# Sparse attention with an ELU layer: score blocks in pairs, fills placed in the order, the last tile in three pieces, and zero matmuls during batch 0

## The chip, the cores and the metric

One core of a Trainium2 chip runs the whole program. The metric is the device time of one execution in microseconds, the median of several runs. Engines are named as in the profile: PE (TensorE, its weight loads PEld), DVE (VectorE), ACT (ScalarE), POOL (GpSimd), SP (SyncE).

## What is computed

```python
def attn(q, k, v):                      # (8, 8, 576, 64): batch, heads, tokens, head size
    scores = np.matmul(q, k.transpose(0, 1, 3, 2)) / np.sqrt(64)
    rel = pos[:, None] - pos[None, :]
    local   = (rel >= 0) & (rel < 32)                      # heads 0 to 3
    strided = (rel >= 0) & (pos[None, :] % 32 == pos[:, None] % 32)   # heads 4 to 7
    return softmax(where(mask, scores, -1e9)) @ v
x = attn(q, k, v).transpose(0, 2, 1, 3).reshape(4608, 512)
h = x @ w_in                            # (4608, 2048)
out = where(h > 0, h, exp(min(h, 0)) - 1) @ w_out          # (4608, 512)
```

## The kernel before

**Work.** For each batch, four local and four strided heads are handled as four pairs of heads, called by batch, kind and pair: 0s1 is batch 0, strided, pair 1. Each pair has two score blocks, u = 0 and 1. A block's path: scores (S, PE, line 427, 8 matmuls of 72 columns for strided, 6 of 96 for local), exp (e, ACT, line 434), mask (m, DVE, 441 or 447), values and sums (O, PE, 454 to 499), log of the sums and exp of minus it as reciprocal (n and r, ACT, 525 and 530), and the product into xT (x, DVE, 555), which holds x transposed in four parts of 128 features: parts 2 and 3 come from strided heads, 0 and 1 from local ones.

Batches 0 and 1 get q and k transposed on PE (T, lines 388 and 391, 8 or 16 matmuls) and copied out of PSUM by DVE (c) or ACT (C); later ones by a DMA transpose (X). Two heads of q and of k of batch 0 come as f32 through SP into a stage and are cast (K, line 375: q on DVE, k on ACT).

The layers run in nine chunks of 512 tokens. First layer: 16 blocks of 128 features, each four matmuls of 512 columns (L, line 582), in chunk 0 split in a (parts 2 and 3, strided) and b (parts 0 and 1, local). ELU: exp (h, ACT, 590), clamp (i on DVE, 599, or j on ACT, 597), maximum into g (g, DVE, 608 or 610). Second layer: four tiles of 128 tokens for each chunk, 16 matmuls each, issued in four parts of four (Z, line 616), copied out (o on ACT, q on DVE, 622) and stored (t, SP, 634, one DMA for each run of tokens). One tile, 7.3, is done in two halves of 256 columns at the end (Y and y, lines 638 to 660).

**Order.** ORDER (lines 35 to 143) is a text of tokens; the loop at its end runs one token after the other, and so fixes each engine's instruction order. Semaphores make an instruction wait for its data, and everything behind it on its engine waits too. T.0s0.q.7 is the transposes of q for pair 0s0 into PSUM bank 7; S.0s0.1.01 the scores of block 1 into banks 0 and 1; Z.7.3.1.6 is chunk 7, tile 3, part 1, bank 6. D tokens are loads on POOL's queue (D.wi1.0: the second quarter of w_in, features 512 to 1023; D.wo0: the first quarter of w_out), F tokens fills: F.ms and F.ml build masks on DVE, F.mk on POOL.

Before the order, the program loads the stage, preloads ACT's table, loads the other two strided heads of q and k, and sets constants on DVE: among them ones into both local value buffers vl (lines 308 to 310) and into the strided one vsp (311). The order begins with w.7.42: 42 matmuls of 128 x 128 x 128 on zeros (line 369), into columns that nothing reads.

In batch 0 PE's order is w, T.0s0.q, T.0s0.k, T.0l0.k, T.0s1.k, S.0s0.1, T.0l1.q, S.0s0.0, T.0l1.k, O.0s0.1, T.0l0.q, O.0s0.0, T.0s1.q, six score blocks, six O, T.1s1.q, T.1s0.q, and then six a and the first b, b.0.4. The end is Z.8.3.3, Y.7.3.0, y.7.3.0, Y.7.3.1, y.7.3.1, o.8.3, t.8.3.

Of the kernel before, what the change touches and what calls it, by code (L numbers as in the profile page):

```python
# [15 lines left out]
S = 576  # L16
D = 64
HG = 4
NS = 8
RS = S // NS  # L20
# [4 lines left out]
PRE = STRIDE  # L25
CHUNK = 512
W = S // 2
# [8 lines left out]
w.7.42 D.kl.0 D.ql.0 D.vs.0 K.q.1 D.vl.0 K.q.0 T.0s0.q.7 D.wi2.0 K.k.0 D.qs.1 K.k.1 D.wi1.0 T.0s0.k.6  # L36
c.0s0.k c.0s0.q D.wi3.0 T.0l0.k.5 F.ms T.0s1.k.7 S.0s0.1.01 D.wi0.0 C.0s1.k T.0l1.q.6 e.0s0.1 F.mk
S.0s0.0.23 C.0l1.q m.0s0.1 T.0l1.k.7 D.kl.1 e.0s0.0 O.0s0.1.41 C.0l1.k m.0s0.0 D.ks.1 T.0l0.q.6 c.0l0.k
O.0s0.0.70 C.0l0.q F.ml T.0s1.q.3 n.0s0.0 n.0s0.1 S.0l1.1.56 c.0s1.q r.0s0.1 D.vl.1 e.0l1.1 S.0s1.1.01
V.0 S.0s1.0.23 r.0s0.0 m.0l1.1 S.0l0.1.56 e.0s1.1 e.0l0.1 m.0s1.1 S.0l1.0.01 e.0s1.0 m.0l0.1 S.0l0.0.56  # L40
x.0s0.1 D.ql.1 e.0l1.0 m.0s1.0 O.0l1.1.32 x.0s0.0 e.0l0.0 O.0s1.0.41 n.0l1.1 O.0l0.1.70 m.0l0.0 D.wo0.0
r.0l1.1 m.0l1.0 O.0s1.1.26 n.0s1.0 x.0l1.1 r.0s1.0 O.0l1.0.51 n.0s1.1 x.0s1.0 r.0s1.1 O.0l0.0.63 n.0l0.1
x.0s1.1 n.0l1.0 T.1s1.q.4 D.vs.1 T.1s0.q.0 r.0l1.0 c.1s1.q a.0.7.2 n.0l0.0 a.0.11.1 r.0l0.1 a.0.4.4
C.1s0.q x.0l0.1 a.0.8.3 x.0l1.0 r.0l0.0 a.0.10.7 x.0l0.0 D.wo1.0 a.0.12.5 b.0.4 b.0.8 h.0.4 b.0.10 h.0.8
b.0.11 j.0.4 b.0.7 i.0.8 D.wo2.0 h.0.10 a.0.0.6 g.0.8 a.0.1.0 h.0.7 g.0.4 b.0.1 h.0.11 i.0.10 a.0.6.3
D.wo3.0 h.0.1 i.0.7 b.0.0 j.0.11 g.0.7 b.0.6 h.0.0 b.0.12 g.0.10 j.0.1 a.0.15.4 D.qs.2 g.0.11 a.0.9.7
h.0.12 g.0.1 b.0.9 h.0.6 T.1s0.k.2 i.0.12 h.0.9 b.0.15 c.1s0.k a.0.3.1 i.0.6 j.0.9 b.0.3 D.ks.2 g.0.12
h.0.15 T.1l0.k.2 i.0.0 h.0.3 a.0.2.5 g.0.9 C.1l0.k b.0.2 D.vs.2 g.0.6 a.0.5.0 j.0.3 a.0.13.7 g.0.0 h.0.2
b.0.5 j.0.15 g.0.3 b.0.13 j.0.2 g.0.15 S.1s0.1.23 T.1l0.q.6 e.1s0.1 g.0.2 T.1l1.k.1 D.kl.2 T.1l1.q.4
C.1l0.q c.1l1.k S.1s0.0.23 a.0.14.5 h.0.5 m.1s0.1 Z.0.3.0.6 e.1s0.0 c.1l1.q V.1 h.0.13 T.1s1.k.4 i.0.5  # L50
S.1l0.0.12 c.1s1.k b.0.14 e.1l0.0 m.1s0.0 S.1s1.1.34 m.1l0.0 Z.0.0.0.2 e.1s1.1 g.0.5 h.0.14 S.1s1.0.34
j.0.13 O.1l0.0.10 Z.0.3.1.6 e.1s1.0 g.0.13 m.1s1.1 S.1l1.0.34 i.0.14 Z.0.0.1.2 e.1l1.0 m.1s1.0 n.1l0.0
g.0.14 O.1s1.1.74 r.1l0.0 O.1s0.0.30 m.1l1.0 n.1s1.1 Z.0.3.2.6 x.1l0.0 n.1s0.0 r.1s0.0 r.1s1.1
S.1l1.1.01 x.1s0.0 S.1l0.1.45 e.1l1.1 Z.0.0.2.2 x.1s1.1 e.1l0.1 m.1l1.1 O.1l1.0.73 m.1l0.1 O.1l1.1.54
n.1l1.0 O.1s0.1.10 X.qs.2 n.1l1.1 Z.0.3.3.6 r.1l1.0 r.1l1.1 x.1l1.0 O.1s1.0.43 x.1l1.1 X.ks.2 Z.0.0.3.2
n.1s1.0 n.1s0.1 r.1s0.1 O.1l0.1.75 r.1s1.0 x.1s0.1 Z.0.1.0.3 n.1l0.1 x.1s1.0 r.1l0.1 Z.0.1.1.3 x.1l0.1
W.2 L.1.7.7 D.vs.3 L.1.1.5 X.kl.2 h.1.7 D.ql.2 o.0.3 L.1.0.4 t.0.3 L.1.2.6 h.1.0 j.1.7 i.1.0 L.1.4.1
h.1.1 g.1.0 L.1.6.0 D.qs.3 g.1.7 i.1.1 D.ks.3 L.1.8.4 h.1.6 g.1.1 D.vl.2 h.1.2 L.1.14.7 h.1.4 i.1.2
i.1.6 o.0.0 Z.0.1.2.3 i.1.4 h.1.8 g.1.4 Z.0.1.3.3 h.1.14 g.1.2 D.ql.3 S.2s0.0.12 L.1.10.5 e.2s0.0 j.1.14
m.2s0.0 L.1.5.6 g.1.6 h.1.10 O.2s0.0.12 g.1.14 L.1.3.0 n.2s0.0 i.1.8 g.1.8 Z.0.2.0.7 h.1.5 r.2s0.0  # L60
i.1.10 X.ql.2 Z.0.2.1.7 j.1.5 x.2s0.0 h.1.3 L.1.9.4 o.0.1 i.1.3 g.1.10 S.2s0.1.12 t.0.1 L.1.13.3 e.2s0.1
h.1.9 m.2s0.1 Z.0.2.2.7 t.0.0 h.1.13 g.1.5 O.2s0.1.12 i.1.13 L.1.11.6 X.ks.3 i.1.9 n.2s0.1 g.1.13
Z.0.2.3.7 h.1.11 X.qs.3 r.2s0.1 i.1.11 L.1.12.5 g.1.3 o.0.2 L.1.15.3 g.1.11 h.1.12 x.2s0.1 Z.1.0.0.0
h.1.15 g.1.9 D.ql.4 j.1.12 Z.1.0.1.0 g.1.12 S.2s1.1.12 i.1.15 S.2l0.1.67 S.2s1.0.45 e.2s1.1 Z.1.0.2.0
g.1.15 e.2l0.1 m.2s1.1 S.2l0.0.12 m.2l0.1 S.2l1.0.67 e.2l0.0 Z.1.0.3.0 e.2l1.0 m.2l0.0 O.2l0.1.12 q.1.0
Z.1.2.0.3 e.2s1.0 n.2l0.1 t.1.0 m.2s1.0 Z.1.2.1.3 m.2l1.0 r.2l0.1 O.2l1.0.45 t.0.2 O.2s1.0.67 x.2l0.1
n.2l1.0 Z.1.1.0.0 n.2s1.0 X.ql.3 O.2l0.0.12 Z.1.1.1.0 r.2l1.0 r.2s1.0 x.2l1.0 Z.1.2.2.3 n.2l0.0 D.ks.4
x.2s1.0 S.2l1.1.45 r.2l0.0 D.kl.3 Z.1.1.2.0 e.2l1.1 O.2s1.1.67 Z.1.2.3.3 m.2l1.1 n.2s1.1 x.2l0.0
Z.1.1.3.0 r.2s1.1 O.2l1.1.12 D.qs.4 q.1.1 Z.1.3.0.5 n.2l1.1 D.kl.4 x.2s1.1 Z.1.3.1.5 r.2l1.1 o.1.2
x.2l1.1 S.3s1.0.67 e.3s1.0 S.3s0.1.34 S.3s1.1.01 L.2.2.2 m.3s1.0 W.3 L.2.4.7 h.2.2 e.3s0.1 i.2.2 L.2.9.6  # L70
e.3s1.1 g.2.2 O.3s1.0.34 h.2.4 L.2.0.1 h.2.9 i.2.4 D.vs.4 L.2.11.2 i.2.9 h.2.0 g.2.4 D.vl.3 n.3s1.0
L.2.10.0 m.3s1.1 g.2.9 X.kl.3 r.3s1.0 L.2.3.7 h.2.10 x.3s1.0 L.2.6.6 j.2.0 X.ks.4 i.2.10 h.2.3 g.2.10
O.3s1.1.34 h.2.11 Z.1.3.2.5 g.2.0 h.2.6 L.2.12.0 i.2.11 g.2.11 Z.1.3.3.5 h.2.12 i.2.6 i.2.3 n.3s1.1
L.2.7.2 g.2.3 j.2.12 g.2.6 L.2.1.1 o.1.3 m.3s0.1 L.2.5.7 g.2.12 r.3s1.1 t.1.3 h.2.1 x.3s1.1 S.3s0.0.56
X.qs.4 L.2.8.0 e.3s0.0 i.2.1 h.2.7 m.3s0.0 L.2.13.6 h.2.8 g.2.1 t.1.1 h.2.5 L.2.14.5 i.2.7 h.2.13 g.2.7
X.kl.4 L.2.15.1 j.2.5 i.2.13 i.2.8 h.2.14 O.3s0.0.23 g.2.5 Z.2.1.0.4 n.3s0.0 t.1.2 i.2.14 g.2.8
Z.2.1.1.4 r.3s0.0 X.ql.4 h.2.15 x.3s0.0 Z.2.3.0.7 j.2.15 g.2.13 O.3s0.1.23 g.2.14 Z.2.1.2.4 n.3s0.1
g.2.15 r.3s0.1 S.3l0.0.56 D.qs.5 W.4 Z.2.3.1.7 e.3l0.0 D.vs.5 m.3l0.0 S.3l0.1.01 S.3l1.1.56 e.3l0.1
x.3s0.1 Z.2.3.2.7 D.vl.4 e.3l1.1 m.3l0.1 O.3l0.0.01 Z.2.1.3.4 m.3l1.1 n.3l0.0 O.3l0.1.23 r.3l0.0 D.ks.5
q.2.1 Z.2.0.0.6 D.kl.5 n.3l0.1 x.3l0.0 Z.2.0.1.6 r.3l0.1 O.3l1.1.01 x.3l0.1 Z.2.0.2.6 n.3l1.1 r.3l1.1  # L80
S.4s0.0.23 Z.2.3.3.7 e.4s0.0 x.3l1.1 S.3l1.0.45 S.4s0.1.23 m.4s0.0 S.4s1.1.01 e.4s0.1 Z.2.0.3.6 e.3l1.0
m.4s0.1 Z.2.2.0.3 o.2.3 m.3l1.0 e.4s1.1 q.2.0 O.3l1.0.45 Z.2.2.1.3 n.3l1.0 m.4s1.1 D.ql.5 O.4s1.1.67
r.3l1.0 Z.2.2.2.3 n.4s1.1 x.3l1.0 O.4s0.0.01 Z.2.2.3.3 r.4s1.1 n.4s0.0 x.4s1.1 O.4s0.1.45 L.3.11.2
n.4s0.1 L.3.4.7 r.4s0.0 r.4s0.1 x.4s0.0 L.3.1.6 h.3.11 x.4s0.1 X.ks.5 h.3.4 L.3.2.1 i.3.4 L.3.9.0 g.3.4
h.3.2 t.2.1 j.3.11 i.3.2 S.4s1.0.45 L.3.8.7 h.3.9 g.3.2 X.kl.5 e.4s1.0 g.3.11 L.3.3.1 j.3.9 q.2.2 h.3.1
L.3.13.2 m.4s1.0 t.2.2 h.3.8 i.3.1 O.4s1.0.34 h.3.3 g.3.1 L.3.5.5 t.2.3 n.4s1.0 g.3.9 L.3.0.6 h.3.13
i.3.8 t.2.0 g.3.8 j.3.3 L.3.7.0 h.3.0 i.3.13 X.qs.5 h.3.5 g.3.13 L.3.6.7 j.3.0 g.3.3 L.3.12.2 j.3.5
g.3.0 X.ql.5 r.4s1.0 L.3.10.1 g.3.5 h.3.7 x.4s1.0 Z.3.2.0.6 h.3.6 i.3.7 h.3.12 S.4l0.1.34 g.3.7
Z.3.0.0.5 j.3.6 j.3.12 g.3.6 L.3.14.0 e.4l0.1 h.3.10 Z.3.0.1.5 m.4l0.1 h.3.14 i.3.10 O.4l0.1.34 g.3.12
L.3.15.7 n.4l0.1 i.3.14 g.3.10 Z.3.2.1.6 r.4l0.1 W.5 h.3.15 S.4l1.1.12 x.4l0.1 Z.3.0.2.5 D.vs.6 e.4l1.1  # L90
D.kl.7 j.3.15 m.4l1.1 S.4l1.0.12 S.4l0.0.34 g.3.14 Z.3.2.2.6 e.4l0.0 e.4l1.0 O.4l1.1.34 Z.3.1.0.0
n.4l1.1 m.4l1.0 g.3.15 O.4l1.0.12 r.4l1.1 Z.3.1.1.0 D.ql.6 n.4l1.0 x.4l1.1 Z.3.1.2.0 r.4l1.0 m.4l0.0
Z.3.2.3.6 x.4l1.0 O.4l0.0.34 Z.3.0.3.5 n.4l0.0 D.vl.5 r.4l0.0 S.5s0.0.12 Z.3.1.3.0 e.5s0.0 x.4l0.0
Z.3.3.0.7 m.5s0.0 o.3.1 D.qs.6 o.3.0 O.5s0.0.01 D.ks.6 L.4.7.4 n.5s0.0 D.kl.6 L.4.2.5 o.3.2 r.5s0.0
L.4.3.6 h.4.2 x.5s0.0 L.4.5.3 h.4.3 j.4.2 i.4.3 S.5l1.0.01 L.4.8.2 h.4.5 g.4.3 h.4.7 g.4.2 L.4.1.6 h.4.8
# [51 lines left out]
def kernel(  # L147
# [9 lines left out]
    nc = tc.nc  # L157
# [550 lines left out]
```

## Time and profile before

| | |
|---|---|
| Median of 3 runs | 315.01 us (314.72 to 315.85) |
| Profiled execution | 312.68 us, of it span 310.7 us, mean granted clock 0.974 |
| PE, DVE, ACT, POOL busy | 96%, 71%, 75%, 26% of the span |
| L616 and L582, second and first layer | 135.6 and 132.0 us of PE |
| First L1 matmul, last PE instruction's end | 22.26 us, 305.06 us |
| DMA | 37.59 MB, mean 121 GB/s |

The page cuts the span into 40 slices and gives each engine's busy share in tenths, and the clock that PE was granted. The windows view gives the same for chosen stretches, in us, with the number of instructions in brackets. The timeline has one row for instructions of one kind in a row: start, length, engine, line, operation, how many, and in square brackets the idle time of the engine ahead of them with what ended it. Instructions overlap in a pipeline, so a cost is read from start to start.

### The profile page before, as it was taken

The numbers are of one execution on the slowest core, as the hardware profiler recorded it, in microseconds if no ns is written. First come the engines' busy times: TensorE is split into PE (matmuls) and PEld (weight loads), VectorE is DVE, ScalarE is ACT, GpSimd is POOL, SyncE is SP. The second block draws the span as 40 slices with busy tenths as digits, with TensorE's granted clock in tenths as the row PEclk, the third lists the DMA queues.
The fourth block names the chain that finished last, engine by engine and source line by source line (L and its number), as shares of the span: only waits on it lengthen the run. The fifth ranks groups of instructions, "written<-read, shape, count | busy, mean of one in ns | idle before, by whom it ended". The sixth has DMA issues, their size and how long they took to land.

```text
span 310.7 us, 6213 instructions
## 1 busy us (share of the span) xinstructions
PE 299.0 (96%) x2330; PEld 150.4 (48%) x2330; DVE 219.1 (71%) x422; ACT 234.5 (75%) x421; POOL 79.8 (26%) x107
## 2 busy tenths in 40 slices
PE   6789999999999999999999999999999999999992
PEld 5664544444544445444444454445445544444452
DVE  5467985788579976898398886966797739885200
ACT  3698976687978989998798999987778667843021
POOL 8843320934830065006901640000000000000000
PEclk9569999999999999999999999999999999999998
DMA  8999999999999899666998999603102030100152
GB/s 164 188 206 194 207 207 193 165 165 194 165 167 135 129 209 147 133 163 67 126 174 185 122 87 151 169 14 95 36 1 70 0 101 0 37 0 0 40 165 68
DMA packets 106717, 37.59 MB, mean 121 GB/s; under 512 B 88992, under 2 KB 101888, under 8 KB 106688
## 3 DMA queue, kind: packets, MB, share of 16 engines
q0 software_dynamic: 69600, 19.43, 60.3%
q1 hardware_dynamic: 37008, 17.70, 27.7%
q8 instruction: 18, 0.29, 0.4%
q14 instruction: 11, 0.09, 0.1%
q10 hardware_dynamic: 80, 0.07, 0.1%
HBM read 39.47 MB, written 9.44 MB: 157 GB/s over the span
## 4 chain that ended last, share of the span: by engine, by line
PE 87%; DVE 4%; ACT 3%; DMA 2%; issue 1%; POOL 1%; ACTq 0%; POOLq 0%
PE ps L616 38%; PE ps L582 38%; PE ps L427 4%; DMA ql<-in_q_dram 2%; PE ps L490 2%; PE ps L497 2%; DVE g L608 1%; PE ps L642 1%; ACT e L434 1%; DVE he L599 1%; DVE g L610 1%; PE ps L391 1%; PE ps L470 1%; ACT ln L525 0%; ACT osb L622 0%
## 5 line engine op out<-in xcount | busy, mean ns | idle before, releaser
L616 PE MATMUL ps<-w_out_sb,g 128*128 128x512 bf16 x560 | 135.6, 380 | 0.0
L582 PE MATMUL ps<-xT,w_in_sb 128*128 128x512 bf16 x576 | 132.0, 379 | 0.0
L590 ACT ACTIVATE he<-ps 128x512 f32<-128x512 f32 x144 | 80.4, 596 | 24.7 <-PE ps L582 24.1
L582 PEld LDWEIGHTS <-w_in_sb 128*128 128x128 bf16 x576 | 54.5, 98 | 63.1 <-issue 0.6
L616 PEld LDWEIGHTS <-g 128*128 128x128 bf16 x560 | 50.4, 98 | 53.8 <-DVE g L610 0.4
L610 DVE TENSOR_TENSOR g<-he,ps 128x512 bf16<-128x512 bf16 x89 | 59.5, 683 | 1.3
L555 DVE TENSOR_TENSOR xT<-ps,ln 64x576 bf16<-64x576 f32 (+1 forms) x64 | 42.9, 678 | 23.9 <-ACT ln L530 22.0
L599 DVE TENSOR_SCALAR he<-he 128x512 bf16<-128x512 f32 x89 | 38.3, 439 | 14.6 <-ACT he L590 13.8
L434 ACT ACTIVATE e<-ps 72x576 bf16<-72x576 f32 (+1 forms) x64 | 39.8, 646 | 7.8 <-PE ps L427 6.8
L525 ACT ACTIVATE ln<-ps 64x576 f32<-64x576 f32 (+1 forms) x64 | 36.7, 582 | 8.3 <-PE ps L497 3.8
L608 DVE SCALAR_TENSOR_TENSOR g<-he,ps 128x512 bf16<-128x512 bf16 x55 | 36.9, 682 | 8.4 <-ACT he L597 8.0
L530 ACT ACTIVATE ln<-ln 64x576 f32<-64x576 f32 (+1 forms) x64 | 39.2, 620 | 1.6
L597 ACT ACTIVATE he<-he 128x512 bf16<-128x512 f32 x55 | 33.8, 628 | 2.7 <-DVE g L610 1.2
L236 POOL DMA_DIRECT2D ql<-in_q_dram x24 | 20.0, 840 | 11.6 <-DMA qTl<-ql 9.6
L441 DVE TENSOR_TENSOR pm<-e,mask_s 72x576 bf16<-72x576 bf16 x32 | 14.4, 449 | 9.6 <-ACT e L434 9.4
L622 ACT COPY osb<-ps 128x512 f32<-128x512 f32 x18 | 10.3, 583 | 13.4 <-PE ps L616 10.4
L243 POOL DMA_DIRECT2D kl<-in_k_dram x24 | 17.6, 759 | 7.4 <-DMA w_out_sb<-in_moe_w_out_dram 4.6
L447 DVE TENSOR_TENSOR pm<-e,mask_l 128x576 bf16<-128x576 bf16 x32 | 14.4, 454 | 6.0 <-ACT e L434 5.6
L622 DVE COPY osb<-ps 128x512 f32<-128x512 f32 x17 | 11.6, 688 | 7.1 <-PE ps L616 6.5
L230 POOL DMA_DIRECT2D vs<-in_v_dram x7 | 4.7, 671 | 39.8 <-DVE vsp L562 38.9
L253 POOL DMA_DIRECT2D vl<-in_v_dram x8 | 10.1, 1259 | 8.0 <-PE ps L497 6.6
L490 PEld LDWEIGHTS <-vsp 72*128 72x128 bf16 x192 | 9.2, 98 | 5.1 <-DVE pm L441 0.2
(85 smaller groups left out, 161.4 us busy)
## 6 DMA issues: line engine op xcount, KB each, us to landing
out_dram<-osb SPq DMA_DIRECT2D x32, 144.0 KB
vl<-in_v_dram POOLq DMA_DIRECT2D x8, 288.0 KB, 8.4
w_in_sb<-in_moe_w_in_dram POOLq DMA_DIRECT2D x4, 512.0 KB, 14.5
w_out_sb<-in_moe_w_out_dram POOLq DMA_DIRECT2D x4, 512.0 KB, 16.2
vs<-in_v_dram POOLq DMA_DIRECT2D x6, 320.0 KB, 7.1
kl<-in_k_dram POOLq DMA_DIRECT2D x24, 72.0 KB, 7.2
ql<-in_q_dram POOLq DMA_DIRECT2D x24, 72.0 KB, 5.2
qs<-in_q_dram POOLq DMA_DIRECT2D x5, 320.0 KB, 7.2
```

The costliest lines, as they stand in the source:

```text
L434: nc.scalar.activation(e[0:R], tiles.pop(("S", key, u))[0:R], ACT.Exp, scale=scale)
L525: nc.scalar.activation(t, s_ps, ACT.Ln)
L530: nc.scalar.activation(t, t, ACT.Exp, scale=-1.0)
L555: nc.vector.tensor_mul(dst, o_ps, rc)
L582: nc.tensor.matmul(tiles["h", ch, m], lhsT=w_in_sb[:, c, m * 128:(m + 1) * 128], rhs=xT[:, c, ch * CHUNK:(ch + 1) * CHUNK], start=(c == 2) ...
L590: nc.scalar.activation(e, tiles["h", i[0], i[1]], ACT.Exp)
L597: nc.scalar.activation(e1, e, ACT.Relu, bias=1.0, scale=-1.0)
L599: eng.tensor_scalar(e1, e, scalar1=1.0, scalar2=1.0, op0=ALU.min, op1=ALU.subtract)
L608: nc.vector.scalar_tensor_tensor(dst, e1, -1.0, h, op0=ALU.mult, op1=ALU.max)
L610: nc.vector.tensor_tensor(dst, e1, h, op=ALU.max)
L616: nc.tensor.matmul(ops, lhsT=g[ch % 2][:, m, kk * 128:(kk + 1) * 128], rhs=w_out_sb[:, m, :], start=(m == 0), stop=(m == MC - 1), skip_gro ...
L622: eng(o_sb, tiles.pop(("o", int(ch), int(kk))))
```

## The change

The order is written anew as a whole, for every batch, with other banks. What differs in kind:

- **Start.** w.7.42 becomes w.7.46, and nine more w tokens (102 zero matmuls) stand between the work of batch 0. PE's order there is now w 46, T.0s0.q, w 26, T.0s0.k, T.0s1.k, w 12, S.0s0.0, T.0s1.q, S.0s0.1, w 7, S.0s1.0, S.0s1.1, w 12, O.0s0.1, O.0s0.0, T.0l1.k, T.0l0.k, T.0l1.q, T.0l0.q, w 8, S.0l1.1, S.0l1.0, w 9, O.0s1.0, O.0s1.1, S.0l0.0, S.0l0.1, w 15, O.0l1.0, w 2, O.0l1.1, w 11, a.0.5, a.0.7, O.0l0.1, O.0l0.0, five a, b.0.7. The transposes of batch 1 all come later.
- **Loads.** vs0 goes ahead of kl, ql and vl; then wi1, wi0, wi2, qs1, wi3, wo0, wo1, ks1, kl1, wo2, ql1, wo3, vs1, vl1.
- **Fills.** The ones in vsp and in the second vl become tokens F.vp and F.v1, between the first loads. One small memset for each kT (32 columns) is new.
- **Casts.** One half of q goes to ACT and one half of k to DVE (token k beside K).
- **Pairs.** From batch 1 on every score block stands in a row with exactly one other.
- **Copies of the second layer.** 23 on DVE and 12 on ACT, where it was 17 and 18.
- **Last tile.** 7.3 in pieces of 256, 128 and 128 columns; the first is copied by ACT, the others by DVE, and the stores of the last two are issued by SP and ACT, one DMA each. Tile 8.3 is copied and stored earlier; the order ends with Y.7.3.0, o.8.2, t.8.2, y.7.3.0, Y.7.3.1, y.7.3.1, Y.7.3.2, y.7.3.2.

```diff
-w.7.42 D.kl.0 D.ql.0 D.vs.0 K.q.1 D.vl.0 K.q.0 T.0s0.q.7 D.wi2.0 K.k.0 D.qs.1 K.k.1 D.wi1.0 T.0s0.k.6
-c.0s0.k c.0s0.q D.wi3.0 T.0l0.k.5 F.ms T.0s1.k.7 S.0s0.1.01 D.wi0.0 C.0s1.k T.0l1.q.6 e.0s0.1 F.mk
...
+w.7.46 D.vs.0 F.vp D.kl.0 F.v1 D.ql.0 k.q.1 K.q.0 D.vl.0 F.ms T.0s0.q.7 D.wi1.0 k.k.0 K.k.1 D.wi0.0
+C.0s0.q w.3.26 T.0s0.k.6 T.0s1.k.5 C.0s0.k D.wi2.0 C.0s1.k D.qs.1 w.3.12 S.0s0.0.67 T.0s1.q.4 e.0s0.0
+S.0s0.1.01 c.0s1.q e.0s0.1 w.5.7 S.0s1.0.23 D.wi3.0 S.0s1.1.45 m.0s0.1 m.0s0.0 F.mk e.0s1.1 w.3.12
...
-    for t in vl_t:
+    def fill_vloc(t):
         fill_ones(t, HG * LB)
         nc.vector.memset(blocks(t, HG * LB)[0:PRE, 0, :], 0.0)
-    fill_ones(vs_p, HG * NS)
+
+    fill_vloc(vl_t[0])
...
         nc.vector.memset(t["l"][:, 0:PRE], 0.0)
+        nc.vector.memset(t["l"][:, S:S + PRE], 0.0)
...
+        elif what == "vp":
+            fill_ones(vs_p, HG * NS)
+        elif what == "v1":
+            fill_vloc(vl_t[1])
...
-    def l2_half(ch, kk, i, bk):
+    def piece(i):
+        f = d_model // 4
+        return (0, 2 * f) if i == "0" else ((1 + int(i)) * f, (2 + int(i)) * f)
+
+    def l2_piece(ch, kk, i, bk):
+        f0, f1 = piece(i)
+        ops = tiles["o", ch, kk, i] = ps[:, int(bk), 0:f1 - f0]
...
+                rhs=w_out_sb[:, m, f0:f1],
...
+        (nc.scalar.copy if i == "0" else nc.vector.tensor_copy)(
+            o_sb[:, f0:f1], tiles.pop(("o", ch, kk, i)))
+        store(ch, kk, (nc.sync,) if i == "0" else (nc.sync, nc.scalar), slice(f0, f1))
```

## The prediction

> **What bounds the kernel now.** I read the page's 40 slices first, then the windows of the start, then TensorE's (PE's) timeline at the start, in the middle and at the end, then the waits. From the page:
>
> ```profile
> PE   6789999999999999999999999999999999999992
> PEclk9569999999999999999999999999999999999998
> ```
>
> PE is full from the fourth slice of 7.8 us to the last one; only the first three and the last one have holes, and the same first slices show the clock at half. A busy PE is not proof of a full PE, so I checked its pace in the middle (timeline of PE):
>
> ```profile
> 127.77 0.30 PE L427 MATMUL ps<-qTs,kTs 64*128 64x72 bf16 x8
> 128.00 2.77 PE L582 MATMUL ps<-xT,w_in_sb 128*128 128x512 bf16 x12
> ...
> 143.13 0.43 PE L427 MATMUL ps<-qTl,kTl 64*128 64x96 bf16 x12
> 143.49 1.04 PE L616 MATMUL ps<-w_out_sb,g 128*128 128x512 bf16 x4
> ```
>
> From start to start, twelve 512-column matmuls take 2.59 us or so, 0.2157 each, so a token L or Z (four) takes 0.863. The waits of PE after 22 us sum to 0.7 us in two places. So from the first L1 matmul (22.26) on, time is PE's own work, and what other engines save there is worth nothing. What can be gained is: an earlier full stage, less PE work in it, a shorter end.
>
> The start, by windows (the numbers of interest are PE's busy time, its instructions and PEclk, the third number from the end):
>
> ```profile
> 4.50:7.90 3.40, 1.73 (x28) 1.19 (x25) 1.58 (x7) 1.14 (x2) 3.40 (x6) 1.00 1.22 193
> 7.90:11.30 3.40, 1.90 (x42) 1.55 (x44) 0.82 (x4) 0.74 (x2) 3.04 (x6) 0.50 1.23 191
> 11.30:14.70 3.40, 3.40 (x84) 2.94 (x78) 1.91 (x6) 3.14 (x7) 2.73 (x3) 0.50 1.88 181
> 14.70:18.10 3.40, 2.41 (x44) 1.65 (x44) 2.61 (x6) 3.37 (x8) 2.19 (x2) 0.50 1.25 205
> 18.10:21.50 3.40, 3.25 (x52) 2.83 (x51) 2.55 (x7) 3.23 (x8) 0.78 (x2) 0.50 1.24 207
> ```
>
> Two things stand there. The clock is full to 7.9 and half until 21.5. And from 11 us on ScalarE (ACT) is the engine without a hole (3.14, 3.37, 3.23 of 3.40): exps, logs, reciprocals and copies of batch 0 run one behind the other, and end with the last reciprocal at 24.23. Before that, ACT is empty, because PE's order puts a transpose of kl (T.0l0.k) ahead of the first scores:
>
> ```profile
> 6.90 0.30 PE L388 MATMUL ps<-identity,ks 72*128 72x72 bf16 x4 [0.22 <-ACT ks L375]
> 9.24 0.69 PE L391 MATMUL ps<-identity,kl 72*64 72x72 bf16 x16 [2.03 <-DMA kl<-in_k_dram]
> 9.86 0.66 PE L388 MATMUL ps<-identity,ks 72*128 72x72 bf16 x8
> 10.45 0.42 PE L427 MATMUL ps<-qTs,kTs 64*128 64x72 bf16 x8
> ```
>
> The strided q and k were in place at 8.07 (DVE's copies of 7.24 and 7.62); the scores came at 10.45.
>
> **Part 1, the start: -3.1 us.** The new order puts everything strided first and the kl transposes after O.0s0. Walk, at full clock: 46 zero matmuls instead of 42 (starts 107 ns apart up to 4.5 us, then 56) end at 5.3; T.0s0.q 5.3; w.3.26, 26 x 0.056 = 1.46, to 7.0, where T.0s0.k could have gone at 6.45 (cast on DVE after F.ms), so these overrun by 0.55; T.0s0.k ends 7.5; ACT's copy (0.64) 8.1; scores 8.25 to 8.7; first exp 8.7, against 11.09 now. From its first exp to its last reciprocal ACT needed 13.14 us for 8 exps, 8 logs, 8 reciprocals, 4 copies, nearly without a hole. The same stretch now has 2 copies, each worth 0.53 start to start: 12.1. The two fills that move into the order (F.vp 1.0, F.v1 0.9) are on DVE before K.q.0 as before, 4.54 to 4.7; nothing.
>
> Loads: vs0 now goes first, and loads land one behind the other, 1.6 to 1.9 us for a q, k or v, 2.4 to 2.9 for a weight quarter (wi2: issued 6.34, 10.7 us to landing; kl 9.2, ql 11.0, vs 12.7). So kl lands near 10.8 and ql near 12.5. T.0l1.k comes at 11.3 (covered), T.0l1.q at 12.1, so PE waits 0.4 and ACT's chain slips some 0.5: last reciprocal 8.7 + 12.1 + 0.5 = 21.3, write of xT (0.46) 21.8. First b (needs the local half of xT): 21.8, with seven a's done by then; now 24.86, with six. wi1 lands where wi2 did (17.05), wi0 at 19.6 against a need at 20.2, wi2 22.2 (24.8), wi3 26.4 (27.4), wo2 37.2 (38.5), wo3 41.4 (42.6), vs1 43.3 (44.8). Cover is about a microsecond everywhere: a later load costs its lateness, an earlier PE gains nothing more. The gain of the first b is 24.86 - 21.8 = **3.06**.
>
> The other 102 zero matmuls (5.7 us at 56 ns) stand in PE's queue in front of T, S and O of batch 0. That work is about 8 us at full clock, so PE has 14 us of work in the 16.5 from 5.3 to 21.8, and ACT stays last. At half clock they cost 107 ns and the cover is gone (rival B). They are bounded below by nothing (all in waits) and above by 10.9 us (all on the path at half clock); I take the 0.55 of the walk, since most stand where PE waits for an exp.
>
> Will the clock stay? The window that lost it had 1.73 busy of 3.4 us; the one that regained it 3.25. In the new order zero matmuls, T and S fill the window from 4.5 to some 3.3. That is nearer to the second. The window 11.30:14.70, though, was busy throughout and did not regain it; 48 of its 84 matmuls are transposes. The Trainium skill, TensorE: Matmul & The Clock Gate (part 4, on the PE transpose), says that transposes don't count as busy, and part 1 that the gate judges windows of 3.4 us; the trace agrees with both (4.5 to 7.9, and 13.65 us at half, four such windows). By that rule the first window would count 2.3 us of zero matmuls instead of 3.3, between lost and regained, which speaks against the full clock; the sum would then be rival B's.
>
> **Part 2, PE's work from the first b on: -1.0 us.** A single score block between large matmuls costs 0.23 and makes the matmuls before it 0.10 longer (126.81's four take 0.96, not 0.86); each further one in a row costs 0.14. So 0.2 for each run. Batches 2 to 7 have 30 runs now and 24 pairs after (48 blocks both times), batch 1 has 7 and 4: with the neighbours counted 14.64 becomes 13.09, -1.55. One a-token less lies behind the first b (-0.43). Four transposes of batch 1 that ran before it, or stood next to one another, now stand singly: 2.09 to 3.00, +0.91. Last tile: 16 matmuls of 256 columns (1.75) become 32 of 128 at 56 ns, +0.05. Sum: -1.02. Work after the first b is then 276.6, by rows; the same sum for the kernel before is 277.6, while it took 24.86 to 304.90, 280.0. So 2.4 us are lost in small waits (b.0.14 0.43, Z.0.1.3.3 0.3, S.3s1.0 0.25 and so on). I keep 2.4 for the new order; bounds 0.5 and 6. Start of PE's end: 21.8 + 276.6 + 2.4 = 300.8, against 304.9: **-4.1** for parts 1 and 2.
>
> **Part 3, the end: -1.9 us.**
>
> ```profile
> 305.09 0.27 ACT L658 COPY osb<-ps 128x128 f32<-128x128 f32 x1 [1.33 <-PE ps L642]
> 305.39 0.29 DVE L659 COPY osb<-ps 128x128 f32<-128x128 f32 x1 [12.00 <-ACT osb L658]
> 305.71 0.55 ACTq L634 DMA_DIRECT2D out_dram<-osb  x1
> 306.36 0.58 ACT L622 COPY osb<-ps 128x512 f32<-128x512 f32 x1 [1.00 <-DMA out_dram<-osb]
> ```
>
> PE ends at 305.06. Two copies of one bank go one behind the other, ACT issues a store (0.55), and only then copies tile 8.3, which SP stores until 307.7. Span's end 310.7: 3.0 us after the last issue. In the new order 8.3 is done long before, and after PE's end come one copy of 128 columns (0.29, ready 0.32 after it) and two stores issued side by side (0.55): 0.9 instead of 2.65. That is 1.75, and 0.15 for the smaller last transfer. If SP is still busy with earlier stores: 0.4 less.
>
> **Sum.** -4.1 - 1.9 = -6.0 us. Profiled execution: 312.68 (span 310.7, 1.98 around it) becomes 306.7. The median of the runs is 315.01, 2.3 above the profiled one; with the same difference 309.0.
>
> **Rivals.**
> A: the front is held by loads. If one load more lies ahead of each first need, kl, wi0 and wo come 1.7 to 2.9 us later and PE waits for them. For: 1 us of cover, loads land at some 200 GB/s without a hole up to 90 us. Against: the order of loads follows the new needs. Gain of part 1 mostly lost: 311.5.
> B: the clock drops after all. Each window at half clock takes 1.7 us of PE's work; 2.5 us of cover. With two windows 1 to 2.5 us lost, about 311; in all of batch 0, PE's 14 us become 25 and the first b is at 29, 7 later: 316, no change.
> C, the other side: pairs make PE wait. A pair holds four banks instead of two until ACT has done two exps (0.646 each). If PE reaches each second pair one exp too early, 14 x 0.646 = 9.0 us: 318.0, slower. It decides from 0.27 us for each of 28 pairs on (7.5 us). For: ACT is busy 90% between 80 and 200 us. Against: the three blocks in a row at 74.92 and 203.72 hold six banks now and cost no wait; only 88.23 waited, 0.25.
> D: the change does not do what it says: zero matmuls in front of work that is ready, fills as late as before. Start unchanged, part 2's 1.0 and part 3 remain: 312.1, less what the zero matmuls take; 313.5.
>
> **Chances.** Forecast 0.52 (307 to 310.5); A and B's mild case 0.22 (310.5 to 313.4); D and B's full case 0.14 (313.4 to 316.6); C 0.12. Faster by over 0.5% (about what measurement tells from no change, 1.6 us) 0.74, within it 0.14, slower 0.12. The range reaches from losses of 0.5 (minus 1.9, and half a microsecond of the end) to where 0.2 are left out: 306.2 to 314.5.
>
> **What would show it.** First exp near 8.7, first b near 21.8, PEclk full from 4.5 on; PE's last matmul about 301 and the span's end 3.7 after it (5.6 now). Wrong: half clock between 8 and 20, PE waits on w_in_sb or w_out_sb loads, PE waits for exps ahead of score pairs, or more than 6 us between 276.6 and the time that the full stage takes.

## The result, and the profile after

The changed kernel takes 310.44 us in the median (309.92 to 311.33, 4 runs) against 314.87 for the kernel before beside it (314.08 to 315.85). The ratio is 0.9861, with a 95% interval of 0.9823 to 0.9898: 4.4 us or 1.4% less, clear of the noise, where 6.0 were forecast and 309.0 as the time. The time lies inside the range, 1.4 above the forecast. But of the three parts of the sum one is right in its total, one was put at twice its size and one missed almost whole. By luck the profile that the sum started from was a short execution, which gave back 2 of the 3.5 us that were missing.

The two profiles side by side. The tail is the time from the end of PE's last matmul to the end of the span.

| | before | after | difference | forecast |
|---|---|---|---|---|
| profiled execution, us | 312.68 | 310.17 | -2.5 | -6.0 |
| span | 310.7 | 308.5 | -2.2 | |
| first exp | 11.09 | 9.69 | -1.4 | 8.7 |
| first b (part 1) | 24.86 | 23.44 | -1.42 | -3.06 |
| first b to PE's end (part 2) | 280.20 | 279.55 | -0.65 | -1.02 |
| tail (part 3) | 5.60 | 5.47 | -0.13 | -1.9 |

The page after, PE and its granted clock in the 40 slices: the first slices, which showed 6, 7, 8 and the clock at half, are full now, and the last one is as empty as before.

```profile
PE   8999999999999999999999999999999999999992
PEclk9999999999999999999999999999999999999999
```

The windows of the start after the change (busy us of PE, PEld, DVE, ACT, POOL with instructions, then granted clock, DMA share, GB/s). PE is busy nearly throughout, and no step down of the clock is left in this execution, as forecast. (Three other executions with the same start do have one, below.) (The clock's column starts at 1.00 in every profile; the slow beginning isn't in it and is read off the pace of the zero matmuls, 107 ns apart ahead of the first rise and 56 behind it.) ACT, though, has holes again (1.62, 2.42, 2.74 of 3.4).

```profile
4.50:7.90 3.40, 3.40 (x48) 3.40 (x46) 2.02 (x8) 1.62 (x3) 3.40 (x6) 1.00 1.14 184
7.90:11.30 3.40, 3.40 (x86) 2.96 (x84) 0.79 (x2) 2.42 (x4) 3.27 (x6) 1.00 1.29 201
...
18.10:21.50 3.40, 3.10 (x43) 1.89 (x43) 2.28 (x6) 2.74 (x8) 0.75 (x1) 1.00 1.24 205
```

PE's timeline at the start after the change. The 46 zero matmuls last to 5.94, not 5.3: they ran 107 ns apart throughout, since the clock rose only at 6.78 in this execution. The 26 that follow took 1.6 us from start to start instead of 1.46, T.0s0.k came at 8.05 instead of 7.0, and the first scores at 9.34 instead of 8.25.

```profile
1.06 5.09 PE L376 MATMUL ps<-zero 128*128 128x128 bf16 x46 [1.06 <-DVE zero L293]
5.94 0.69 PE L394 MATMUL ps<-identity,qs 72*128 72x72 bf16 x8
6.44 1.78 PE L376 MATMUL ps<-zero 128*128 128x128 bf16 x26
8.05 0.68 PE L394 MATMUL ps<-identity,ks 72*128 72x72 bf16 x16
...
9.34 0.30 PE L433 MATMUL ps<-qTs,kTs 64*128 64x72 bf16 x8
...
18.59 0.51 PE L376 MATMUL ps<-zero 128*128 128x128 bf16 x6
19.39 0.45 PE L376 MATMUL ps<-zero 128*128 128x128 bf16 x5 [0.30 <-issue]
19.68 1.03 PE L588 MATMUL ps<-xT,w_in_sb 128*128 128x512 bf16 x4
...
21.27 4.92 PE L588 MATMUL ps<-xT,w_in_sb 128*128 128x512 bf16 x22
```

The last rows are the 11 zero matmuls of w.7.11, a.0.5 and a.0.7, and then the five a's with the first b behind them (the view ends at 26 us).

In the middle the pairs look as planned: sixteen score matmuls in 0.37 us from start to start, none waiting, and eight of the first layer behind them.

```profile
66.45 0.43 PE L433 MATMUL ps<-qTs,kTs 64*128 64x72 bf16 x16
66.82 2.15 PE L588 MATMUL ps<-xT,w_in_sb 128*128 128x512 bf16 x8
```

The end after the change, in three views: the copies and ACT's stores, SP's last two stores, and the row of what SP's queue waited for (total us, times, longest). PE ends at 302.99, and DVE's last copy at 303.39.

```profile
302.14 0.29 DVE L662 COPY osb<-ps 128x128 f32<-128x128 f32 x1 [6.26 <-PE ps L652]
302.46 1.45 ACTq L640 DMA_DIRECT2D out_dram<-osb  x2
303.10 0.29 DVE L662 COPY osb<-ps 128x128 f32<-128x128 f32 x1 [0.67 <-PE ps L652]
```

```profile
304.53 1.11 SPq L640 DMA_DIRECT2D out_dram<-osb  x2
```

```profile
SPq L640 <- DMA out_dram<-osb: 1.7, 1, 1.7
```

ACT issues its stores of the last two pieces from 302.46 on. SP, which was to issue beside it, does nothing from 302.75 to 304.53, and then issues two stores one behind the other. It waits 1.7 us for a DMA of out_dram, one that ACT had issued: in the trace's records SP's wait, which ends at 304.50, is for the semaphore that ACT's store of 302.46 counts on, and SP's next store counts on the same one.

### The profile page after: what moved, and what is told of

Read it like the earlier page. It is cut to its first block, busy times and chain, and to the rows that moved or that the text cites. A ratio compares the mean times of both kernels' runs of the same rounds, so it can differ in the third digit from the quotient of the medians.

```text
span 308.5 us, 6465 instructions
## 1 busy us (share of the span) xinstructions
PE 300.1 (97%) x2452; PEld 154.0 (50%) x2452; DVE 224.9 (73%) x432; ACT 231.1 (75%) x413; POOL 78.9 (26%) x107
## 4 chain that ended last, share of the span: by engine, by line
PE 86%; DVE 4%; ACT 3%; DMA 3%; issue 1%; POOL 1%; POOLq 0%; DVEq 0%; ACTq 0%
PE ps L622 39%; PE ps L588 35%; PE ps L433 3%; DMA ql<-in_q_dram 3%; PE ps L503 2%; PE ps L496 2%; ACT he L596 1%; PE ps L652 1%; PE ps L376 1%; DVE he L605 1%; ACT he L603 1%; DVE g L616 1%; DVE g L614 1%; ACT e L440 1%; PE ps L397 1%
## 5 line engine op out<-in xcount | busy, mean ns | idle before, releaser
L622 PE MATMUL ps<-w_out_sb,g 128*128 128x512 bf16 x560 | 133.4, 379 | 0.3 <-DVE g L614 0.3
L622 PEld LDWEIGHTS <-g 128*128 128x128 bf16 x560 | 51.1, 98 | 55.2 <-issue 0.4
L440 ACT ACTIVATE e<-ps 72x576 bf16<-72x576 f32 (+1 forms) x64 | 39.1, 646 | 10.8 <-PE ps L433 9.2
L605 DVE TENSOR_SCALAR he<-he 128x512 bf16<-128x512 f32 x90 | 39.0, 442 | 8.2 <-ACT he L596 7.4
L628 DVE COPY osb<-ps 128x512 f32<-128x512 f32 x23 | 15.7, 685 | 11.6 <-PE ps L622 11.1
L237 POOL DMA_DIRECT2D ql<-in_q_dram x24 | 19.6, 822 | 7.7 <-DMA w_out_sb<-in_moe_w_out_dram 4.3
L628 ACT COPY osb<-ps 128x512 f32<-128x512 f32 x12 | 7.0, 586 | 13.5 <-PE ps L622 13.5
L376 PE MATMUL ps<-zero 128*128 128x128 bf16 x148 | 12.7, 251 | 1.4 <-DVE zero L293 1.1
```

The lines of the kernel that those rows point to most:

```text
L440: nc.scalar.activation(e[0:R], tiles.pop(("S", key, u))[0:R], ACT.Exp, scale=scale)
L605: eng.tensor_scalar(e1, e, scalar1=1.0, scalar2=1.0, op0=ALU.min, op1=ALU.subtract)
L622: nc.tensor.matmul(ops, lhsT=g[ch % 2][:, m, kk * 128:(kk + 1) * 128], rhs=w_out_sb[:, m, :], start=(m == 0), stop=(m == MC - 1), skip_gro ...
L628: eng(o_sb, tiles.pop(("o", int(ch), int(kk))))
```

## Experiments

The theory after the result: (1) SP's wait for a landing is what took part 3's gain away; (2) the start lost 1.6 of the forecast 3.06 to a cold beginning, to fills that collide, and to a's placed in front of the last O; (3) the zero matmuls are worth nothing measurable. The rivals: the pairs or the loads took the gain; the zeros hold the clock and so carry it; the profile of before was no typical execution.

**The zeros, taken out of the changed kernel (e1).**

```diff
-C.0s0.q w.3.26 T.0s0.k.6 ... D.qs.1 w.3.12 S.0s0.0.67 ... e.0s0.1 w.5.7 S.0s1.0.23 ...
+C.0s0.q T.0s0.k.6 ... D.qs.1 S.0s0.0.67 ... e.0s0.1 S.0s1.0.23 ...
```

All nine w tokens behind w.7.46 go; they feed nothing.

> The changed kernel without the nine rows of zero matmuls inside batch 0 (the 46 at the start stay). Theory 1 (the zeros hold the clock): the granted clock falls to half some 3.4 us after the first zeros end and comes back between 17 and 24 us; transposes, scores and values of batch 0 run at half rate, the first b comes at 23.5 to 26 us instead of 23.4, and the time is 1 to 3 us above the changed kernel's 310.4, with a wider spread of runs. Rival (the early start comes from the order of the work alone and the zeros only stand in PE's way): first b at 22.5 or earlier, time 309.5 or less.

Measured: 309.69 us (309.55 to 310.85), ratio 0.9855 (0.9839 to 0.987), against 0.9861 for the change. The clock dropped at 10.96 and stayed at half until 21.2, yet the first b came at 23.65, 0.2 later than in the profile after and 1.35 earlier than in a second one (e11, below), and the first scores at 7.83, 1.5 earlier. So the clock fell as theory 1 says, without the longer time that it forecast, and the rival's first b of 22.5 did not come either. What the zeros gain in clock they cost in two ways that the traces show. They stand in PE's queue in front of work that is ready: in the profile after, DVE had written the last strided product at 18.69, but a.0.5 started at 19.68, behind the zeros of w.7.11. And some zeros go into a bank that a block's scores have just filled (w.4.9 behind S.0l1.0.34), so that the block's exp waits for them too. In the executions where the clock fell, ACT waited for such zeros: 0.7 us in e2, 2.4 in e4, and 1.1 in e11, whose row of waits is

```profile
ACT e L440 <- PE ps L376: 1.1, 2, 0.7
```

**The zeros alone, in the kernel before (e3).**

```diff
-T.0s0.k.6 ... T.0s1.k.7 S.0s0.1.01
+T.0s0.k.6 w.4.34 ... T.0s1.k.7 w.4.8 S.0s0.1.01 w.4.8
```

> The kernel before with 34 zero matmuls behind T.0s0.k (where PE waits for kl) and 8 each behind T.0s1.k and S.0s0.1; nothing else changed. Theory 1 (the clock alone is worth little, since ACT is last in batch 0; it takes away the unlucky runs): clock full to 11 us or longer, first b within 0.5 of 24.9, time 313 to 315. Rival (the clock is most of the gain): first b at 23.5 or earlier and time near 311.5.

Measured: 314.0 us (12 runs, 312.74 to 315.8), ratio 0.9988 (0.9967 to 1.0008). The clock's half stage began at 14.36 instead of 7.89 and still ended only at 24.6; first b 26.21, 1.3 later than theory 1 has it, though within what the kernel before shows without zeros (24.86 to 27.57, below). No measurable worth on this side either.

**Stores of the last pieces on SP alone (e2).**

```diff
-        store(ch, kk, (nc.sync,) if i == "0" else (nc.sync, nc.scalar), slice(f0, f1))
+        store(ch, kk, (nc.sync,), slice(f0, f1))
```

> The changed kernel with all stores of the last tile's pieces issued by SP, none by ACT. Theory 1 (SP's store of the second piece waited 1.7 us for the landing of a store that ACT had issued, because both count on one completion semaphore): no such wait, SP issues one store behind the other, the last at about 304.9 minus the first b's shift, span's end 5.5 us after PE's end becomes 4.7; time 0.7 lower, 309.7. Rival (the end is set by the landing of the earlier, larger stores): the distance from PE's end to the span's end stays at 5.5.

Measured: 309.9 us (308.71 to 312.54), ratio 0.9862 (0.983 to 0.9895). SP's queue shows no wait for a DMA at this line any more, and the tail is 5.02 instead of 5.47 (4.7 expected): the wait was real. But SP is busy without a hole from 302.43 to 306.10 with six stores of about 0.6, so most of the tail stays. What the wait cost can only be estimated, since no run has three pieces on two queues without it: in the profile after SP was free at 302.75 and the last copy ended at 303.39, so that the last issue could have ended near 304.0 instead of 305.63. That is 1.6 of the 1.8 us that part 3 missed; six issues on one queue give most of it away again.

**The pairs split (e4).** In 27 of the 28 pairs of batches 1 to 7 the second block is moved behind the next L, Z, a or b token.

```diff
-S.2s1.0.01 S.2s1.1.23 i.1.2 D.ql.3 h.1.14 L.1.11.5
+S.2s1.0.01 i.1.2 D.ql.3 h.1.14 L.1.11.5 S.2s1.1.23
```

> The changed kernel with 27 of the 28 score pairs of batches 1 to 7 split: the second block stands behind the next token of the first or second layer. Theory 1 (each run of score blocks costs PE 0.2 us beyond the blocks themselves): 27 x 0.2 = 5.4 us more PE time, 315.8. Rival (the pairs' gain is eaten by waits for banks, so that splitting gives it back): within 1.5 us of 310.4.

Measured: 324.24 us (323.19 to 325.59), ratio 1.0301 (1.0282 to 1.0319), 13.8 more than the change. From the first b to PE's end it takes 292.5 instead of 279.55. The order has 49 runs of score blocks instead of 28, so the prediction's rows (0.23 and 0.10 for a run, less 0.14 for a further block) give 4.0 of these 12.9. The other 8.9 are mostly waits: behind 28 us PE's sum to 8.3, against 1.1 in the profile after. PE's timeline shows some:

```profile
71.83 1.04 PE L582 MATMUL ps<-xT,w_in_sb 128*128 128x512 bf16 x4
73.17 0.31 PE L427 MATMUL ps<-qTs,kTs 64*128 64x72 bf16 x8 [0.31 <-ACT e L434]
73.72 1.02 PE L582 MATMUL ps<-xT,w_in_sb 128*128 128x512 bf16 x4 [0.24 <-DVE g L610]
...
75.72 1.02 PE L582 MATMUL ps<-xT,w_in_sb 128*128 128x512 bf16 x4 [0.74 <-ACT e L434]
```

This order was made by moving blocks only, with the banks of the paired order, so the waits say what splitting costs here and not what a best order with single blocks would cost; the 0.2 for each run is not tested by it. Rival C is answered by the profile after: of the 1.1 us that PE waits there, none stands in front of scores.

**Tile 8.3 early, alone in the kernel before (e5).**

```diff
-... Z.8.3.3 ... Y.7.3.0 y.7.3.0 Y.7.3.1 y.7.3.1 o.8.3 t.8.3
+... Z.8.3.3 ... Y.7.3.0 o.8.3 t.8.3 y.7.3.0 Y.7.3.1 y.7.3.1
```

> The kernel before with tile 8.3 copied and stored ahead of the last tile's first copy; nothing else changed. Theory 1 (the end of the kernel before was late because 8.3 stood behind the last tile): PE's end as before, span's end 4.2 us after it instead of 5.6, time 1.4 lower, about 313.1. Rival (the end is set by something else, such as the landings of the last tile): distance stays at 5.6, time unchanged.

Measured: 311.86 us (311.28 to 312.63), ratio 0.993 (0.9903 to 0.9957). The tail is 3.84 against 5.60 (4.2 expected): -1.8, nearly all that part 3 was to give, from this one move. Its last issue ends at 306.65, 1.2 after PE's end (305.44):

```profile
306.09 0.56 ACTq L628 DMA_DIRECT2D out_dram<-osb  x1
```

**The fill of ql's spare rows moved from POOL to DVE (e6), and without the zeros (e7).** In the change POOL sets these rows in F.mk, beside DVE's copy of the mask.

```diff
-            nc.gpsimd.memset(odd["ql"][64:RP], 0.0)      # in F.mk
+        elif what == "q0":                               # token F.q0 behind k.k.0
+            nc.vector.memset(odd["ql"][64:RP], 0.0)
```

> The changed kernel with the memset of the 16 spare rows of ql taken from POOL's F.mk and put on DVE behind k.k.0, where DVE is idle. Theory 2 (DVE's copies of F.ml were stretched from 0.36 us to 1.04 and in other runs 2.00, because POOL's memset of 1.80 us ran beside them, and with them c.0l0.k, c.0l1.q and PE's next step came late): the two copies take 0.36 again, PE does not wait behind T.0l0.q, first b 0.6 to 1.6 earlier than in the same order with the memset on POOL (23.4 and 24.8 there), time 309.0 to 309.8. Rival (the copies are slow for another reason, such as the DMAs of these microseconds): copies stay above 0.8 and the time at 310.4.

> As the run with the moved memset, and without the nine rows of zero matmuls inside batch 0. Theory 2 with zeros that are worth nothing either way: within 0.6 us of the run with the moved memset. Rival (with DVE no longer late, PE's clock decides batch 0): 0.8 us or more slower than it.

Measured: e6 309.79 us (308.84 to 311.85), ratio 0.9874 (0.9842 to 0.9906); e7 309.67 us (309.19 to 310.02), ratio 0.9858 (0.9832 to 0.9883). In the medians neither differs from the change. In the trace the copy is as short as its work again, 0.36 for the two (DVE's timeline in e6), where it was 1.04 in the profile after and 2.00 in a second one of the same kernel (below):

```profile
10.97 0.36 DVE L338 COPY mask_l<-mask 128x288 bf16<-128x288 bf16 x2
```

The first b of e6 is 22.94, 0.5 before the change's, with the clock full from 4.75 on. That isn't the memset's worth alone: in the profile after the clock rose only at 6.78, and e6's first scores came 0.96 earlier. The pair without zeros tells more. e1 and e7 differ in this memset only; the two copies take 2.00 and 0.38, and the medians are 309.69 and 309.67. So the collision is removed, and no gain in time is shown. e7 against e6 is a second test of the zeros: again no worth, and its four runs lie within 0.8 us.

**Both kernels again, unchanged (e9, e10, e11),** since the change had gained 4.4 in the medians and 2.5 between the profiles.

> The kernel before, unchanged, for a second profile of it. Theory 3 (the profile that the prediction was worked out from was a fast execution of the kernel before: the granted clock changes in steps that run free of the program, so the length of batch 0 differs from run to run): first b later than 24.86 by 0.3 to 2, full stage 280.0 to 280.3, distance from PE's end to the span's end 5.6; the span follows the first b. Rival (the time moves in the full stage or the end): first b within 0.2 of 24.86, another stage longer.

> The kernel before, unchanged, a third profile. Theory 3: as for the one ahead of it; with another moment of the clock's steps another first b, the full stage and the end as always. Rival: first b the same in all three, another stage moves.

> The changed kernel, unchanged, for a second profile of it. Theory 3: first b between 22.9 and 25, full stage 278.5 to 279.5, distance 5.5. Theory 2: DVE's two copies of F.ml take 1.0 to 2.0 us beside POOL's memset. Rival (the zeros hold the clock in every run): full clock from its first release to the end, first b within 0.3 of 23.4.

Measured, each one execution, in us:

| | time | first scores | clock full / half / full | first b | first b to PE's end | tail |
|---|---|---|---|---|---|---|
| before | 312.68 | 10.45 | 4.48 / 7.89 / 21.55 | 24.86 | 280.20 | 5.60 |
| e9, before | 314.84 | 9.57 | 6.15 / 9.56 / 26.63 | 27.28 | 279.99 | 5.62 |
| e10, before | 315.15 | 9.88 | 6.18 / 9.60 / 26.66 | 27.57 | 280.02 | 5.63 |
| after | 310.17 | 9.34 | 6.78 / - / - | 23.44 | 279.55 | 5.47 |
| e11, after | 311.12 | 8.39 | 4.28 / 14.52 / 17.93 | 25.00 | 278.92 | 5.49 |

The last two columns hardly move. The first b of the kernel before moves by 2.7, and with it the whole time: the profile of the prediction was an execution in which the clock came back early. All steps of the clock are multiples of 3.41 us apart (3.41, 6.83, 10.24, 13.65, 17.07), and the first one falls differently in each execution. Three more executions have one of these two starts: the first b came at 25.22 in e5 (before's), 24.83 in e2 and 25.88 in e4 (the change's). The windows laid along these steps, first of before, then of e10, show how 1.7 us in phase made 5.1 in the return, one whole window more:

```profile
18.13:21.55 3.42, 3.27 (x52) 2.80 (x51) 2.52 (x7) 3.25 (x8) 0.83 (x2) 0.50 1.24 206
```

```profile
19.84:23.25 3.41, 3.25 (x51) 2.70 (x48) 2.48 (x6) 3.28 (x10) 0.68 (x2) 0.50 1.24 207
23.25:26.66 3.41, 3.19 (x8) 1.21 (x8) 1.28 (x3) 1.32 (x4) 0.75 (x1) 0.50 1.24 206
```

Before regained the clock with the window of 3.27 busy. In e10 a window with 3.25 did not do it, and one of 3.19 did. One difference is in what PE was busy with. The same first window of e10, line 388 alone (the transposes of batch 1; PE, PEld, clock, DMA share, GB/s):

```profile
19.84:23.25 3.41, 1.14 (x16) 0.97 (x16) 0.50 1.24 207
```

So 1.14 of the 3.25 are transposes; in before those transposes begin at 21.62, after the window. This alone doesn't decide it, as e3, e4, e5 and e8 show (under "Will the clock stay?" below). From 23.75 e10 ran its first 512-column matmuls at half rate, 0.43 us from start to start instead of 0.2157, until 26.66.

In e11 PE lost the clock in one window, 11.11 to 14.52, with 1.88 busy of 3.41. Here is why PE had that hole, from the timelines of DVE, POOL and PE:

```profile
11.43 2.00 DVE L343 COPY mask_l<-mask 128x288 bf16<-128x288 bf16 x2 [0.59 <-POOL mask L337]
```

```profile
11.46 1.80 POOL L340 MEMSET ql<- 16x2048 bf16 x1
```

```profile
13.15 0.96 PE L397 MATMUL ps<-identity,ql 72*64 72x72 bf16 x32 [1.06 <-DMA ql<-in_q_dram]
14.56 1.01 PE L376 MATMUL ps<-zero 128*128 128x128 bf16 x8 [0.45 <-DVE kTl L409]
```

PE waits 1.06 for the load of ql and 0.45 for DVE's copy kTl, which stands behind the mask copies. The two ended at 13.35 and 13.43, 0.09 and 0.17 after POOL's memset of 1.80 us; without such a neighbour they take 0.36 (e6). The load landed no later than in the profile after (13.11 and 13.16); PE came to it 0.95 sooner, because its clock had risen 2.5 us sooner.

**The last tile in two halves (e8, e12).** Both with e7's start. e8 stores each half on SP; e12 copies the second half on ACT and DVE and stores it on SP and ACT.

```diff
-        f = d_model // 4
-        return (0, 2 * f) if i == "0" else ((1 + int(i)) * f, (2 + int(i)) * f)
+        f = d_model // 2
+        return int(i) * f, (int(i) + 1) * f
...
-        store(ch, kk, (nc.sync,) if i == "0" else (nc.sync, nc.scalar), slice(f0, f1))
+        store(ch, kk, (nc.sync,), slice(f0, f1))
```

> As the run before it, and the last tile in two halves of 256 columns, the second copied by DVE in one, all stores by SP. Theory 1: no store waits for another engine's, two issues of 0.5 after PE's end instead of four; span's end 4.3 us after PE's end (5.5 with the three pieces), time 1.2 lower than the run before it, 307.5 to 308.5. Rival (the two more pieces shorten the end by making the last transfer small): distance 5.0 or more, as with three pieces by SP alone.

> The changed kernel without zero matmuls inside batch 0, with the memset on DVE, and the last tile in two halves; the second half copied in two by ACT and DVE and stored by SP and ACT, as in the kernel before. Theory 1 (two stores issued side by side on two engines, with no completion semaphore in common, beat two on one engine): distance 3.8 to 3.9 instead of 4.2, time 0.3 to 0.4 below the version with all stores on SP, 307.5. Rival (the two copies of one bank, one behind the other, cost what the second queue saves): distance 4.2, same time.

Measured: e8 307.94 us (307.52 to 308.02), ratio 0.9801 (0.9776 to 0.9826), tail 4.24; e12 307.76 us (306.97 to 308.25), ratio 0.9771 (0.9744 to 0.9797), tail 4.07. Against e7 (309.67, tail 5.47) both gain at least what their tails say: 1.2 and 1.4 in the tail, 1.7 and 1.9 in the medians. These are the fastest versions here, some 2.6 us faster than the change (310.44); the intervals of the two overlap, and e12's tail lies between the 3.8 to 3.9 of its theory and the rival's 4.2, so that two queues beat one is not shown. The end of e12: two copies, each queue one issue, no wait for a landing.

```profile
302.50 0.27 ACT L662 COPY osb<-ps 128x128 f32<-128x128 f32 x1 [1.38 <-PE ps L646]
302.80 0.29 DVE L663 COPY osb<-ps 128x128 f32<-128x128 f32 x1 [7.42 <-ACT osb L662]
303.13 0.56 ACTq L634 DMA_DIRECT2D out_dram<-osb  x1
```

## Why the prediction was right, and where it was wrong

- **"What bounds the kernel now": right.** From the first b on, time is PE's own work. That stage took 280.0 to 280.4 in the five executions that have before's order there (e3 and e5 among them), whatever the clock had done earlier, and 278.8 to 279.6 in the six with the change's.
- **Part 2 (-1.02): right in its total.** Measured -0.65 between the two profiles and -1.1 in the means of those five and six executions. Its terms, the 0.2 for a run of scores among them, were not tested one by one. The 2.4 us of small waits kept for the new order were about right: 276.6 by rows, 278.8 to 279.6 measured.
- **Part 1 (-3.06): right in direction, twice too large.** Measured -1.42 between the two profiles, and -1.4 in the means of four executions with each start (26.2 and 24.8, spread over 2.7 and 2.4 us). Three steps were off.
  - First, "46 zero matmuls ... end at 5.3": the walk took the clock's first step from one execution (4.48), and it falls anywhere from 3.7 to 6.8. In the profile after, the first exp came at 9.69, 1.0 late; in e11 and e2, where the clock rose at 4.28 and 4.51, it came at 8.74 and 8.77, as forecast.
  - Second, "nearly without a hole": ACT's work from first exp to last reciprocal shrank by 1.25 us (12.65 to 11.40, forecast 1.06), but its holes grew from 0.5 to 1.3 in the profile after and to 3.3 in e11 and e2, where the clock fell. So the stretch took 12.7 in the one, by chance the forecast 12.1 + 0.5, and 15.0 in the others.
  - Third, the walk ended with "write of xT (0.46) 21.8", as if the first b waited only for that. The last reciprocal ended at 22.37, and the first b came 1.07 later: O.0l0 stands behind a.0.5 and a.0.7 and ended at 21.27, and the five a's in front of b.0.7, 0.43 each, last until 23.43. The seven a's that I counted as "done by then" were the thing waited for.
  - What in the new start earns the gain was not isolated: the zeros are ruled out (e1, e3, e7), and the order, the casts and the loads were changed together.
- **"F.mk" beside F.ml: not in the prediction at all.** POOL's memset and DVE's copies met; they cost 0.68 of DVE in the profile after (1.04 instead of 0.36) and 1.64 in e11. With the memset moved, the copies are short again (e6, e7); that this saves time is not shown (e7 against e1).
- **"Will the clock stay?": in part.** It stayed in the profiles of the change and of e6, and fell for one window in e2 and e11 and for two in e4. The mean granted clock of the change's four runs (0.998, 0.997, 0.997 and 0.992, where e11 has 0.992) suggests that it stayed in three of them. The reason given, 3.3 busy of 3.4 early on, held there: along the clock's own steps the two windows up to 11.1 in e11 have 3.36 and 3.42 busy. The loss came in the next one, in a hole that a load and a fill made. The sentence that spoke against the change, that the clock might not count transposes, did not come true for keeping it: the change kept the clock through a window with 3.25 busy, 1.09 of it transposes, and e6 through one with 2.70, 1.26 of it transposes. Where the clock is to be regained, the Trainium skill, TensorE: Matmul & The Clock Gate (Part 4), which doesn't count them, fits before and e10, but not all runs: e8 and e4 had windows of 3.31 and 3.41 without any transpose (13.97 to 17.38, 14.54 to 17.95) and stayed at half, and e3 and e5 regained it with windows of 3.41 that hold 1.14 of transposes. What regains the clock is left open. (The prediction's "48 of its 84 matmuls are transposes" is a misreading, the trace has 56; the argument stays the same.)
- **The zeros at 0.55, bounds 0 and 10.9:** their whole worth, cost and gain together, is nothing that two tests in the changed kernel and one in the old can measure. The cost was larger than 0.55: 1.0 in front of a.0.5 alone in the profile after, and 0.7 to 2.4 in waits of exps where the clock fell. The price that rival B put on half clock in all of batch 0, 7 us, counted the zeros themselves as work: e1, without them, had half clock for 10 us and its first b only 0.2 after that of the profile after.
- **Part 3 (-1.9): failed.** The step that failed is "two stores issued side by side (0.55)", and with it "If SP is still busy with earlier stores: 0.4 less". SP did not issue side by side; it stood 1.7 us in a wait for a store that ACT had issued. The two count on the same completion semaphore, out of eight that the program hands out to the stores of both queues; that the wait goes when all stores are on SP (e2) or when there are fewer of them (e8, e12) fits that, but which stores share one was not shifted by an experiment. Behind the wait came the second thing that I had not priced: a last tile in three pieces needs four issues of 0.5 to 0.6 at its end, two on each queue, where halves need two. The gain that the prediction saw was there: e5 has it with one token moved (-1.8), and the pieces gave it back. The 0.15 for the smaller last transfer was about right: from the last issue to the span's end it took 2.95 before and 2.83 after.
- **"The median ... with the same difference": failed, to the prediction's advantage.** The profiled execution of before was 2.2 to 2.5 below the two taken later, all of it in the first b. So it lay 2.3 under its median, while the one after lies 0.3 under its own, and the gain is 4.4 in the medians against 2.5 between the profiles. Of the 3.5 us that the parts fell short, 2 came back in this way, and 1.4 is the miss that is left: that the time came so near is luck, two errors of opposite sign.
- **Rivals.** A: loads landed within 0.7 of the forecast (after: kl 10.21, forecast 10.8; ql 13.16, forecast 12.5; wi0 19.55, forecast 19.6), and only ql was waited for, 0.2 to 1.06. B: its mild case came in e11, e2 and e4. C: did not come, PE waits for no exp ahead of scores after the change. D: wrong for the whole, since the start and the stage gained, but right that zeros stand in front of work that is ready.

## What to carry to other kernels

Where a profile shows a clock that steps, take two or three profiles before walking a start from one: here the first b of one and the same kernel came up to 2.7 us later in another execution, more than any part of the sum but one. At the end of a kernel count issues for each queue, and look in the queue's own waits for landings of stores that another queue issued: more pieces and more queues may be later than two halves. When an order is rewritten, check for each first need what stands in front of it on PE (here five a's), not only when its data are there, and where filler matmuls are put in, keep them out of banks that another engine is about to read (here exps waited up to 2.4 us for them).

## What was not expected of the hardware

- The clock changes in steps of 3.41 us whose start differs between executions: its first rise fell between 3.74 and 6.78 us in the profiles here. The Trainium skill, TensorE: Matmul & The Clock Gate (Part 1, What's actually happening), says the same, a window of 3413 ns that runs freely, and the traces agree. It ties the loss to an idle window. Here the windows of the start that lost the clock had PE busy for 1.11 to 2.52 us of 3.41 (e10 and e7 at the ends), so a window that is a quarter empty was enough. It was not always: e12, e1, e8 and e3 kept the clock through the window behind its first rise with 2.03, 2.08, 2.10 and 2.37. PE's busy time alone doesn't tell which windows lose it.
- A POOL memset of 16 x 2048 bf16 took 1.80 us, and the first of the DVE copies of 128 x 288 bf16 that met it ended 0.09 us after it, in both executions of the change and in e1, e2 and e4. DVE's mask products beside the same memset kept their 0.45 (after, and before). The Trainium skill, SBUF — State Buffer (SBUF: two separate sides), says that a POOL instruction and a DVE one in a two-port mode need the same pair of ports, which whoever starts first holds for its whole instruction, and that products with two SBUF inputs are blocked only by a POOL operation that reads SBUF. The rows of the change agree; in e11 the record of the first copy begins 0.03 us ahead of the memset and it was held all the same, so the records don't settle who came first.
- A store that ACT issued held up a store on SP for 1.7 us, though neither needed the other's data: the program has both count on one semaphore, and SP waits for the first to land before it issues the second.
